# Attention scores from unrounded float32 q and k, two heads of a pair on two row tiles of TensorE

## The chip, the core and the metric

One core of a Trainium2 chip runs the kernel. The metric is the time of one execution on the device in microseconds (us), the median of several runs.

## The reference, cut to what matters

Attention over 2 batches of 12 heads (448 positions, 64 wide), then two feed-forward layers on the 896 tokens:

```python
scores = scale * np.matmul(q, k.transpose(0, 1, 3, 2))
scores = cap * np.tanh(scores / cap)
attn = np.exp(scores - np.max(scores, axis=-1, keepdims=True))
attn = attn / (np.sum(attn, axis=-1, keepdims=True) + 1e-09)
x = np.matmul(attn, v)              # then (B, H, S, D) -> (B*S, H*D)
h = x @ w_in                        # softmax times h, layer norm, @ w_out
...
(sigmoid(x @ w_gate) * (x @ w_val)) @ w_out
```

## The kernel before

The kernel has two branches, chosen at run time by the size of `cap`. With the cap of 30 of this input it takes the one without a maximum (`general` is False), and only that one is followed here.

**Stages.** Attention comes first, then layer 1 (`x @ w_in`, softmax, layer norm) by tiles of 128 tokens, then layer 2, and last the gated layer. Attention runs in *slots*. There are 12 pairs of heads, and slot `s` handles half of the keys (2 of 4 blocks of 112) of pair `s // 2`. The loop `for s in range(-1, NS)` (line 541) writes out the order of TensorE, VectorE, ScalarE and GpSimd by hand. In iteration `s` come the scores of slot `s + 1` (`s_mm`, line 202), their tanh (`s_tanh`, line 212), the product with v and the row sums of slot `s` (`s_pv`, line 238), the exp of slot `s + 1` (`s_exp`, line 235), and five steps of the weight conversion (`fill`, line 320). After an odd slot, `s_out` (line 265) copies the pair's product (on ScalarE, to `to`) and sums (on VectorE, to `ts`) out of PSUM. Two PSUM buffers hold product and sums, so the next pair's product waits for both copies. `n_recip` and `n_mult` divide by the sums two and four slots later; the reciprocals go out to DRAM and come back broadcast into the first two q and k tiles.

**Scores.** q and k of one head lie in one tile `qk_raw` of 128 partitions by 2 by 448, with the 64 values of the head dimension stored twice, on partitions 0 to 63 and 64 to 127. `s_round` (line 177) rounds both to float32r (`qk_hi`), `s_ql` (line 188) takes the remainder of q (`ql`), and `s_kl` (line 192) puts the remainder of k on the lower 64 partitions of `qk_hi`. Rounding is on VectorE and remainders are on GpSimd, except for the first two heads. A block of scores is then two float32r matmuls over 128 partitions:

```python
nc.tensor.matmul(sc[:KC, c, :S], ks, hi[:, 0], start=True, stop=False)
nc.tensor.matmul(sc[:KC, c, :S], ks, ql, start=False, stop=True)
```

The PSUM pool `big` has three buffers of two banks. Product and sums are plain float32 matmuls on column tiles: two of 64 columns for the two heads, four of 32 columns for the sums (lines 254 and 262). A plain float32 matmul stands in the trace as two MATMUL rows.

**Weights.** The 12 chunks of `w_in` come as 64-bit floats. A chunk has six steps on VectorE (lines 365, 368, 369, 370, 371, 355) with a cast to `wi_hi` on ScalarE (line 352) between the last two. Five steps stand in each slot from 0 to 15.

**Layer 1 beside attention.** From slot 17 on, 12 matmuls of layer 1 (line 421) stand in each slot on TensorE. The order of SyncE, which issues all transfers, is set by the scheduler of the framework.

Of the kernel before, what the change touches and what calls it, by code (L numbers as in the profile page):

```python
# [11 lines left out]
F32R = mybir.dt.float32r  # L12
# [3 lines left out]
ALU = mybir.AluOpType  # L16
# [4 lines left out]
P = 128  # L21
B, H, S, D = 2, 12, 448, 64
NP = H // 2
NH = B * H
NPAIR = B * NP
# [4 lines left out]
KC = 112  # L30
# [42 lines left out]
def f32(ap):  # L73
    return ap.bitcast(F32)
# [6 lines left out]
@with_exitstack  # L81
def fused_kernel(ctx: ExitStack, tc: tile.TileContext, qk, v, cap, w_in, w_mid, g_ln, w_gv, w_fin, outT):
    nc = tc.nc
    sh = Shared()
    const = ctx.enter_context(tc.tile_pool(name="const", bufs=1))
    sh.ps = ctx.enter_context(tc.tile_pool(name="ps", bufs=3, space=PSUM))
    sh.pso = ctx.enter_context(tc.tile_pool(name="pso", bufs=2, space=PSUM))
    sh.wraw = ctx.enter_context(tc.tile_pool(name="wraw", bufs=3, side="right"))
    sh.cvt = ctx.enter_context(tc.tile_pool(name="cvt", bufs=3, side="right"))
    sh.dram = ctx.enter_context(tc.tile_pool(name="dram", bufs=2, space=DRAM))  # L90


    cap_raw = const.tile([P, 1], F32, name="cap_raw")
    nc.sync.dma_start(out=cap_raw, in_=cap)

    def load(n, pool):
        b, hd = divmod(n, H)
        r = pool.tile([P, 2, S], F32, tag="q", name="qk_raw", bufs=2 if pool is const else N_RAW)
        nc.sync.dma_start(out=r, in_=qk[b, hd])
        return r  # L100

    sh.first = [load(n, const) for n in range(2)]
    sh.load, sh.v = load, v
    cap_neg = const.tile([P, 1], F32, name="cap_neg")
    sh.cap_abs = const.tile([P, 1], F32, name="cap_abs")
    sh.cap_inv = const.tile([P, 1], F32, name="cap_inv")
    nc.vector.tensor_scalar(cap_neg, cap_raw, -1.0, None, ALU.mult)
    nc.vector.tensor_tensor(sh.cap_abs, cap_raw, cap_neg, ALU.max)
    below = const.tile([P, 1], F32, name="below")
    flag = const.tile([P, 1], I32, name="flag")  # L110
    nc.vector.tensor_scalar(below, sh.cap_abs, CAP_FAST, None, ALU.is_le)
    nc.vector.tensor_copy(flag, below)
    nc.vector.reciprocal(sh.cap_inv, sh.cap_abs)
    nc.vector.tensor_scalar(sh.cap_inv, sh.cap_inv, 1.0 / float(D) ** 0.5, None, ALU.mult)
    sh.guard = const.tile([P, 1], F32, name="guard")
    nc.scalar.activation(sh.guard, sh.cap_abs, AF.Exp, scale=-1.0)
    nc.vector.tensor_scalar(sh.guard, sh.guard, EPS, None, ALU.mult)

    sh.ident = const.tile([P, P], F32, name="ident")
    make_identity(nc, sh.ident)  # L120

    warm = sh.ps.tile([P, 2, 512], F32, tag="big", name="warm")
    for c in range(WARM):
        nc.tensor.transpose(warm[:, c // 4 % 2, c % 4 * P:(c % 4 + 1) * P], sh.ident, sh.ident)
    sh.g_sb = const.tile([P, K2], F32, name="g_sb")
    nc.sync.dma_start(out=sh.g_sb, in_=g_ln)
    sh.ones = const.tile([KC, 32], F32, name="ones")
    nc.vector.memset(sh.ones, 1.0)
    sh.mhalf = const.tile([P, 1], F32, name="mhalf")
    nc.vector.memset(sh.mhalf, -0.5)  # L130

    bounded = nc.values_load(flag[:1], min_val=0, max_val=1)
    with tc.If(bounded > 0) as cmp:
        network(tc, sh, False, w_in, w_mid, w_gv, w_fin, outT)
    with cmp.Else():
        network(tc, sh, True, w_in, w_mid, w_gv, w_fin, outT)
# [3 lines left out]
def network(ctx: ExitStack, tc: tile.TileContext, sh, general, w_in, w_mid, w_gv, w_fin, outT):  # L142
    nc = tc.nc
# [4 lines left out]
    def big():  # L148
        t = ps.tile([P, 2, 512], F32, tag="big", name="big")
        return t  # L150
# [17 lines left out]
    a3 = att.enter_context(tc.tile_pool(name="a3" + sfx, bufs=3, side="right"))  # L168
# [2 lines left out]

    raws, qks, vs, es, outs, tos, rs, x_parts = {}, {}, {}, {}, {}, {}, {}, {}


    def s_round(n, split=False):
        qks[n] = (
            a3.tile([P, 2, S], F32R, tag="qk", name="qk_hi", bufs=4),
            a3.tile([P, S], F32R, tag="ql", name="ql", bufs=4),  # L180
        )
        if split:
            nc.scalar.copy(qks[n][0][:, 0], raws[n][:, 0])
            nc.vector.tensor_copy(qks[n][0][:, 1], raws[n][:, 1])
        else:
            nc.vector.tensor_copy(qks[n][0], raws[n])  # L186

    def s_ql(n, eng=nc.gpsimd):
        hi, ql = qks[n]
        eng.tensor_tensor(ql, raws[n][:, 0], f32(hi[:, 0]), ALU.subtract)  # L190

    def s_kl(n, eng=nc.gpsimd):
        hi, _ = qks[n]
        eng.tensor_tensor(hi[D:, 1], raws[n][D:, 1], f32(hi[D:, 1]), ALU.subtract)  # L194

    def v_load(i):
        if i < NPAIR:
# [1 line left out]
            vs[i] = a2.tile([KC, S // KC, P], F32, tag="v", name="v")  # L199
            nc.sync.dma_start(out=vs[i], in_=sh.v[b, hp])  # L200

    def s_mm(n, u):
        hi, ql = qks[n]
        sc = big()
        for c in range(2):
            kc = 2 * u + c
            ks = hi[:, 1, kc * KC:(kc + 1) * KC]
            nc.tensor.matmul(sc[:KC, c, :S], ks, hi[:, 0], start=True, stop=False)  # L208
            nc.tensor.matmul(sc[:KC, c, :S], ks, ql, start=False, stop=True)  # L209
        es[n, u] = sc  # L210

    def s_tanh(n, u):
        e = a3.tile([KC, 2, S], F32, tag="e", name="e", bufs=N_E)
# [261 lines left out]
    order = nullcontext() if general else tc.manual_schedule(engines=ORDERED)  # L475
    order.__enter__()

    def load_qk(n):
        if n < NH:
            raws[n] = sh.load(n, a3)  # L480

    def wi_dst(kk, half):
        c = slice(half * CH, half * CH + CH)
        return lambda: (wi_hi[:, kk, c], wi_lo[:, kk, c], None)

    load_qk(2)
    v_load(0)
    load_qk(3)
    for n in range(2):
        raws[n] = sh.first[n]  # L490
        s_round(n, True)
        s_kl(n, nc.vector)
        s_ql(n, nc.vector if n == 0 else nc.gpsimd)
    chunk_stream([(w_in[:, kk, h * CH:(h + 1) * CH], wi_dst(kk, h), None) for h in range(2) for kk in range(K1)])


# [9 lines left out]
    def phase(slot, k):  # L506
        run(beside.pop((slot, k), []))
# [32 lines left out]
    NS = 2 * NPAIR  # L540
    for s in range(-1, NS):
        m = s + 1
        i, u = divmod(s, 2)
        pair = range(m // 2 * 2, m // 2 * 2 + 2) if m < NS else ()
        for n in pair:
            s_mm(n, m % 2)
        phase(s, 0)
        for n in pair:
            s_tanh(n, m % 2)
        phase(s, 1)  # L550
        if s >= 0 and not general:
            s_pv(i, u)
        elif s >= 0 and u:
            s_pv(i, 0)
            s_pv(i, 1)
        if not general:
            for n in pair:
                s_exp(n, m % 2)
        elif m % 2:
            for n in pair:  # L560
                s_less_max(n)
                s_exp(n, 0)
                s_exp(n, 1)
        if 0 <= s < S_W2:
            fill(FILL)
        elif s == S_W2:
            fill(len(todo))
            w2_stream()
        elif S_W2 < s < S_W2 + 6 and wide:
            fill(s < S_W2 + 6)  # L570
        if u and s > 0 and i < NPAIR - 1:
            s_out(i)
        for n in (2, 3) if m == 0 else (m + 3,):
            if n < NH:
                s_round(n)
                s_ql(n)
                s_kl(n)
                raws.pop(n)
                load_qk(n + 2)
        if u == 0:  # L580
            v_load(i + 1)
        else:
            if i >= 1:
                n_recip(i - 1)
            if i >= 2:
                n_mult(i - 2)
        phase(s, 2)
        phase(s, 3)
# [21 lines left out]
    for t in range(L1_BESIDE, 7):  # L610
# [7 lines left out]
        k = FILL_T if wide else 0  # L618
# [116 lines left out]
    for m in range(DM // P):  # L735
# [3 lines left out]
        for hf in range(2):  # L739
            c = slice(hf * HT, hf * HT + HT)  # L740
# [7 lines left out]

def layouts(np, q, k, v, cap, moe_w_in, moe_w_out, moe_g_ln, moe2_w_gate, moe2_w_val, moe2_w_out):
    c = np.ascontiguousarray  # L750
    qk = np.stack([q, k], axis=2).transpose(0, 1, 4, 2, 3)
    gv = np.stack([moe2_w_gate.reshape(K3, P, K4, P), moe2_w_val.reshape(K3, P, K4, P)])

    def words(a):
        return a.view(np.int64) if a.dtype == np.float64 else a

    return {
        "qk": np.concatenate([qk, qk], axis=2),
        "v": c(v.reshape(B, NP, 2, S // KC, KC, D).transpose(0, 1, 4, 3, 2, 5).reshape(B, NP, KC, S // KC, P)),
        "cap": c(np.broadcast_to(np.asarray(cap).reshape(1, 1), (P, 1))),  # L760
        "w_in": words(c(moe_w_in.reshape(K1, P, F1).transpose(1, 0, 2))),
        "w_mid": words(c(moe_w_out.reshape(K2, P, K3, P).transpose(2, 1, 0, 3))),
        "g_ln": c(moe_g_ln.reshape(K2, P).T),
        "w_gv": words(c(gv.transpose(3, 2, 0, 1, 4).reshape(K4, P, 2 * K3, P))),
        "w_fin": words(c(moe2_w_out.reshape(K4, P, DM // P, P).transpose(2, 1, 0, 3))),
    }
# [15 lines left out]
```

## Time and profile before

| | |
|---|---|
| median of 3 runs | 535.73 us (534.26 to 537.21) |
| profiled execution | 534.95 us, span of its trace 533.2 us |
| TensorE busy | 500.2 us (94%) |
| VectorE busy | 381.3 us (72%) |
| ScalarE busy | 241.7 us (45%) |
| GpSimd busy | 129.0 us (24%) |
| mean DMA rate | 114 GB/s |
| granted TensorE clock | 0.986 of full speed, mean |

PE is TensorE's matmuls, PEld its weight loads, DVE VectorE, ACT ScalarE, POOL GpSimd, SP SyncE. L208 is line 208 of the kernel before. Busy time is a share of the whole span and mixes stages; which engine sets the pace of a stage is read from that stage's window and from the chain of waits. Matmul records overlap, since each has some latency behind its stream; the pace of a row of matmuls is read from their starts.

### The profile page before, as it was taken

How to read it: one execution, taken by the hardware profiler on the slowest of the kernel's cores; microseconds unless marked ns; L12 is line 12 of the kernel's file. 1: busy time of each engine (PE TensorE's matmuls, PEld its weight loads, DVE VectorE, ACT ScalarE, POOL GpSimd, SP SyncE). 2: the span in 40 equal slices, each digit the busy share in tenths (PEclk: the TensorE clock that was granted, in tenths of full speed). 3: DMA queues.
4: the chain of work that ended last, by engine and by line, in shares of the span. 5: the costliest groups of instructions: out<-in, count | busy, mean ns of one | idle time of the engine just before them, and what ended most of it. 6: DMA issues, size and time to landing. Idle time of an engine off the chain costs nothing.

```text
span 533.2 us, 6676 instructions
## 1 busy us (share of the span) xinstructions
PE 500.2 (94%) x2480; PEld 402.3 (75%) x2480; DVE 381.3 (72%) x607; ACT 241.7 (45%) x328; POOL 129.0 (24%) x86
## 2 busy tenths in 40 slices
PE   7879879899999897799999999999999999999996
PEld 6334333366567776689989999999999999999995
DVE  4999999466478888957978888888777776561000
ACT  5979679767624333222446434444333343332000
POOL 3556665874421120000000212221111111000000
PEclk8999889999999999899999999999999999999999
DMA  8757656621010111322555553444443334500001
GB/s 258 228 185 221 197 191 210 182 86 37 18 28 30 39 41 40 120 79 54 184 159 156 160 157 119 118 120 118 120 118 119 106 97 131 153 35 19 36 34 39
DMA packets 20788, 60.57 MB, mean 114 GB/s; under 512 B 3404, under 2 KB 6348, under 8 KB 20748
## 3 DMA queue, kind: packets, MB, share of 16 engines
q1 hardware_dynamic: 20748, 60.07, 36.6%
q8 instruction: 21, 0.34, 0.3%
q14 instruction: 19, 0.16, 0.1%
HBM read 57.18 MB, written 2.79 MB: 112 GB/s over the span
## 4 chain that ended last, share of the span: by engine, by line
PE 72%; DVE 16%; ACT 4%; DMA 4%; issue 2%; POOL 1%; SPq 1%; ACTq 0%; DVEq 0%; POOLq 0%
PE big L658 32%; PE l4o L658 16%; PE l2o L658 10%; PE big L421 6%; PE o L254 3%; DVE cvt L371 2%; DMA qk_raw<-in_qk 2%; DVE cvt L365 1%; DVE cvt L368 1%; DVE cvt L369 1%; DVE wi_lo L355 1%; PE big L208 1%; DMA w_raw<-in_w_in 1%; ACT e L214 1%; DVE qk_hi L186 1%
## 5 line engine op out<-in xcount | busy, mean ns | idle before, releaser
L658 PE MATMUL big<-y_hi,w_hl 128*128 128x448 f32 x576 | 161.7, 362 | 0.0
L658 PEld LDWEIGHTS big<-y_hi,w_hl 128*128 128x128 f32 x576 | 107.9, 187 | 7.9
L658 PE MATMUL big<-y_lo,w_hl 128*128 128x448 f32 x288 | 104.6, 363 | 0.0
L731 POOL TENSOR_TENSOR p_lo<-sg,p_hi 128x896 fp32r<-128x896 f32 x12 | 30.6, 2548 | 209.5 <-ACT p_hi L730 209.5
L658 PE MATMUL l4o<-p_hi,w_hl 128*128 128x448 f32 x288 | 80.7, 361 | 0.0
L352 ACT CAST w_hl<-cvt 128x512 fp32r<-128x512 f32 x66 | 40.8, 618 | 81.0 <-PE big L658 42.7
L371 DVE SCALAR_TENSOR_TENSOR cvt<-w_raw,cvt 128x512 uint32<-128x512 uint32 x78 | 75.6, 971 | 1.2
L355 DVE TENSOR_TENSOR w_hl<-cvt,w_hl 128x512 fp32r<-128x512 f32 x66 | 45.2, 685 | 24.8 <-ACT w_hl L352 24.5
L658 PE MATMUL l2o<-lnhi,w_hl 128*128 128x384 f32 (+1 forms) x192 | 57.0, 374 | 6.3 <-DVE w_hl L355 6.3
L363 ACT ACTIVATE cvt<-w_raw 128x512 f32<-128x512 f32 x54 | 36.2, 670 | 56.2 <-DVE w_hl L355 36.8
L368 DVE TENSOR_SCALAR cvt<-cvt 128x512 f32<-128x512 f32 x78 | 42.1, 540 | 24.3 <-ACT cvt L363 24.2
L370 DVE SCALAR_TENSOR_TENSOR cvt<-w_raw,cvt 128x512 uint32<-128x512 uint32 x78 | 57.7, 740 | 1.4
L658 PEld LDWEIGHTS l4o<-p_hi,w_hl 128*128 128x128 f32 x288 | 54.0, 187 | 3.9
L658 PEld LDWEIGHTS big<-y_lo,w_hl 128*128 128x128 f32 x288 | 54.1, 188 | 3.1
L214 ACT ACTIVATE e<-big,cap_inv 112x896 f32<-112x896 f32 x48 | 46.3, 1009 | 15.7 <-PE big L209 15.6
L658 PE MATMUL l4o<-p_lo,w_hl 128*128 128x448 f32 x144 | 52.3, 363 | 0.0
L254 PE MATMUL o<-e,v 112*64 112x448 f32 x192 | 43.8, 577 | 7.4 <-ACT to L270 2.8
L190 POOL TENSOR_TENSOR ql<-qk_raw,qk_hi 128x448 fp32r<-128x448 f32 x23 | 36.3, 1579 | 47.9 <-DVE r L280 25.6
L236 ACT ACTIVATE e<-e,cap_abs 112x896 f32<-112x896 f32 x48 | 47.4, 1044 | 0.0
L658 PEld LDWEIGHTS l2o<-lnhi,w_hl 128*128 128x128 f32 x192 | 36.3, 193 | 11.6 <-DVE w_hl L355 7.5
L208 PE MATMUL big<-qk_hi 128*112 128x448 f32 x96 | 38.5, 401 | 7.0 <-POOL qk_hi L194 5.5
L369 DVE TENSOR_SCALAR cvt<-cvt 128x512 uint32<-128x512 uint32 x78 | 42.0, 539 | 1.5
(90 smaller groups left out, 651.9 us busy)
## 6 DMA issues: line engine op xcount, KB each, us to landing
w_raw<-in_w_gv SPq DMA_DIRECT2D x36, 512.0 KB
qk_raw<-in_qk SPq DMA_DIRECT2D x24, 448.0 KB
w_raw<-in_w_fin SPq DMA_DIRECT2D x18, 512.0 KB
w_raw<-in_w_in SPq DMA_DIRECT2D x12, 512.0 KB
w_raw<-in_w_mid SPq DMA_DIRECT2D x12, 512.0 KB
v<-in_v SPq DMA_DIRECT2D x12, 224.0 KB
out_t<-ob SPq DMA_DIRECT2D x12, 224.0 KB
qk_raw<-rd SPq DMA_DIRECT2D x22, 112.0 KB
```

What stands on the lines that cost most here:

```text
L190: eng.tensor_tensor(ql, raws[n][:, 0], f32(hi[:, 0]), ALU.subtract)
L208: nc.tensor.matmul(sc[:KC, c, :S], ks, hi[:, 0], start=True, stop=False)
L214: nc.scalar.activation(e, es[n, u][:KC, :, :S], AF.Tanh, scale=sh.cap_inv[:KC])
L236: nc.scalar.activation(es[n, u], es[n, u], AF.Exp, scale=sh.cap_abs[:KC])
L254: nc.tensor.matmul(o[d, :S], vs[i][:, kc, d], e[j][:, c], start=(kc == 0), stop=(kc == 3))
L352: nc.scalar.copy(st["hi"], w)
L355: v.tensor_tensor(st["lo"], st["w"], f32(st["hi"]), ALU.subtract)
L368: word(lambda t, lo, hi: v.tensor_scalar(f32(t), f32(t), as_f32(W_MOST), as_f32(W_LEAST), ALU.min, ALU.max)),
L369: word(lambda t, lo, hi: v.tensor_scalar(t, t, 3, REST, ALU.logical_shift_left, ALU.bitwise_and)),
L370: word(lambda t, lo, hi: v.scalar_tensor_tensor(t, hi, TOP, t, ALU.bitwise_and, ALU.bitwise_or)),
L371: word(lambda t, lo, hi: (v.scalar_tensor_tensor(t, lo, 29, t, ALU.logical_shift_right, ALU.bitwise_or), upper())),
L658: nc.tensor.matmul(out, l, r[kx], start=(first and m == 0), stop=(last and m == 2))
```

## The change

Rounding and remainders are gone, and so are their tiles. A tile `qk_raw` now holds a pair: head 0 on partitions 0 to 63, head 1 on 64 to 127, nothing twice. It has the size of before, so 12 loads of 448 KB take the place of 24. A block of scores of one head is one plain float32 matmul over 64 partitions, and the two heads follow each other on the two halves of the array's rows, each writing another PSUM buffer.

```diff
-    def load(n, pool):
-        b, hd = divmod(n, H)
+    def load(i, pool):
+
+        b, hp = divmod(i, NP)
         r = pool.tile([P, 2, S], F32, tag="q", name="qk_raw", bufs=2 if pool is const else N_RAW)
-        nc.sync.dma_start(out=r, in_=qk[b, hd])
+        nc.sync.dma_start(out=r, in_=qk[b, hp])
         return r
...
-    def s_round(n, split=False):
...
-    def s_ql(n, eng=nc.gpsimd):
...
-    def s_kl(n, eng=nc.gpsimd):
...
-    def s_mm(n, u):
-        hi, ql = qks[n]
-        sc = big()
+    def s_mm(i, u):
+
+        sc = [big(), big()]
+        r = raws[i]
         for c in range(2):
             kc = 2 * u + c
-            ks = hi[:, 1, kc * KC:(kc + 1) * KC]
-            nc.tensor.matmul(sc[:KC, c, :S], ks, hi[:, 0], start=True, stop=False)
-            nc.tensor.matmul(sc[:KC, c, :S], ks, ql, start=False, stop=True)
-        es[n, u] = sc
+            for j in range(2):
+                d = slice(j * D, j * D + D)
+                nc.tensor.matmul(sc[j][:KC, c, :S], r[d, 1, kc * KC:(kc + 1) * KC], r[d, 0], start=True, stop=True)
+        for j in range(2):
+            es[2 * i + j, u] = sc[j]
...
-    load_qk(2)
     v_load(0)
-    load_qk(3)
-    for n in range(2):
-        raws[n] = sh.first[n]
-        s_round(n, True)
-        s_kl(n, nc.vector)
-        s_ql(n, nc.vector if n == 0 else nc.gpsimd)
+    for i in range(2):
+        raws[i] = sh.first[i]
+        load_qk(i + 2)
...
-        for n in pair:
-            s_mm(n, m % 2)
+        if m < NS:
+            s_mm(m // 2, m % 2)
...
-        for n in (2, 3) if m == 0 else (m + 3,):
-            if n < NH:
-                s_round(n)
-                s_ql(n)
-                s_kl(n)
-                raws.pop(n)
-                load_qk(n + 2)
+        if m % 2 and m < NS:
+            raws.pop(m // 2)
+            if m > 3:
+                load_qk(m // 2 + 2)
...
-    qk = np.stack([q, k], axis=2).transpose(0, 1, 4, 2, 3)
+    qk = np.stack([q, k], axis=2).transpose(0, 1, 4, 2, 3).reshape(B, NP, P, 2, S)
...
-        "qk": np.concatenate([qk, qk], axis=2),
+        "qk": c(qk),
```

TensorE's order before, from the product of slot 0 to the sums of slot 1 (the eight rows between them are the scores of slot 2, head by head):

```order
L254 MATMUL o<-e,v 64x448 x4
L262 MATMUL sums<-e,ones 32x448 x4
L208 MATMUL big<-qk_hi 112x448
L209 MATMUL big<-ql,qk_hi 112x448
L208 MATMUL big<-qk_hi 112x448
L209 MATMUL big<-ql,qk_hi 112x448
L208 MATMUL big<-qk_hi 112x448
L209 MATMUL big<-ql,qk_hi 112x448
L208 MATMUL big<-qk_hi 112x448
L209 MATMUL big<-ql,qk_hi 112x448
L254 MATMUL o<-e,v 64x448 x4
L262 MATMUL sums<-e,ones 32x448 x4
```

The same place on TensorE with the change (line 192 is the scores, 238 the product, 246 the sums):

```order
L238 MATMUL o<-e,v 64x448 x4
L246 MATMUL sums<-e,ones 32x448 x4
L192 MATMUL big<-qk_raw 112x448 x4
L238 MATMUL o<-e,v 64x448 x4
L246 MATMUL sums<-e,ones 32x448 x4
```

Eight matmuls of a slot's scores have become four, in the same place; nothing else on TensorE has moved.

VectorE's order before, in slots 3 and 4, from a copy of sums:

```order
L269 COPY ts<-sums 128x448
L186 CAST qk_hi<-qk_raw 128x896
L280 SCALAR_TENSOR_TENSOR r<-r,guard 16x56
L281 RECIPROCAL r<-r 16x56
L370 SCALAR_TENSOR_TENSOR cvt<-w_raw,cvt 128x512
L365 TENSOR_SCALAR cvt<-w_raw 128x512
L355 TENSOR_TENSOR wi_lo<-cvt,wi_hi 128x512
L371 SCALAR_TENSOR_TENSOR cvt<-w_raw,cvt 128x512
L368 TENSOR_SCALAR cvt<-cvt 128x512
L186 CAST qk_hi<-qk_raw 128x896
L369 TENSOR_SCALAR cvt<-cvt 128x512
```

The same place with the change (lines 349 to 355 and 339 are the steps of the conversion, 253 the copy, 264 and 265 the reciprocal):

```order
L253 COPY ts<-sums 128x448
L264 SCALAR_TENSOR_TENSOR r<-r,guard 16x56
L265 RECIPROCAL r<-r 16x56
L354 SCALAR_TENSOR_TENSOR cvt<-w_raw,cvt 128x512
L349 TENSOR_SCALAR cvt<-w_raw 128x512
L339 TENSOR_TENSOR wi_lo<-cvt,wi_hi 128x512
L355 SCALAR_TENSOR_TENSOR cvt<-w_raw,cvt 128x512
L352 TENSOR_SCALAR cvt<-cvt 128x512
L353 TENSOR_SCALAR cvt<-cvt 128x512
```

The casts are gone, and all other steps stand in the order of before.

SyncE's queue before, behind the two loads of the first heads:

```order
L99 DMA qk_raw<-in_qk 128x896
L200 DMA v<-in_v 112x512
L99 DMA qk_raw<-in_qk 128x896
L327 DMA w_raw<-in_w_in 128x1024 x3
L99 DMA qk_raw<-in_qk 128x896
L200 DMA v<-in_v 112x512
L99 DMA qk_raw<-in_qk 128x896 x2
L327 DMA w_raw<-in_w_in 128x1024
```

And with the change, behind the two loads of the first pairs (line 100 is q and k, 182 v, 311 the weights):

```order
L182 DMA v<-in_v 112x512
L100 DMA qk_raw<-in_qk 128x896 x2
L311 DMA w_raw<-in_w_in 128x1024 x3
L182 DMA v<-in_v 112x512
L100 DMA qk_raw<-in_qk 128x896
L311 DMA w_raw<-in_w_in 128x1024
```

v now comes ahead of the third and fourth tile of q and k; as many tiles of q and k as before stand ahead of the first weights, and they now hold eight heads instead of four.

## Rows read from the trace of the kernel before

**Rows 1.** The page: busy us, share of the span and instructions of each engine.

```profile
PE 500.2 (94%) x2480; PEld 402.3 (75%) x2480; DVE 381.3 (72%) x607; ACT 241.7 (45%) x328; POOL 129.0 (24%) x86
```

**Rows 2.** Busy time by stage: window, length, busy us (x instructions), then clock, DMA.

```profile
core 0: us, PE busy (x) PEld busy (x) DVE busy (x) ACT busy (x) POOL busy (x), PEclk, DMA share, GB/s
17.80:79.50 61.70, 50.95 (x259) 21.32 (x256) 61.08 (x80) 47.07 (x57) 39.21 (x25) 0.94 0.61 195
79.50:96.20 16.70, 13.40 (x73) 5.59 (x71) 15.81 (x22) 14.50 (x18) 10.68 (x7) 1.00 0.62 201
96.20:152.00 55.80, 55.40 (x282) 32.08 (x283) 31.24 (x54) 38.16 (x46) 31.41 (x21) 1.00 0.25 74
```

**Rows 3.** The chain of waits in order of time, 17 to 152 us: start, us, what.

```profile
17.77 0.63 DVE qk_hi L186
...
75.46 1.52 DVE cvt L370
...
148.99 2.97 PE big L421 x12
```

**Rows 4.** The timeline from 59.6 us, VectorE and GpSimd: start, us, what.

```profile
59.68 1.20 POOL L194 TENSOR_TENSOR qk_hi<-qk_raw,qk_hi 64x448 fp32r<-64x448 f32 x1
...
59.92 1.25 DVE L369 TENSOR_SCALAR cvt<-cvt 128x512 uint32<-128x512 uint32 x1
...
63.20 0.42 DVE L365 TENSOR_SCALAR cvt<-w_raw 128x512 uint32<-128x512 uint32 x1
```

**Rows 5.** VectorE's groups by form, 18 to 79 us: busy us, mean ns | idle before.

```profile
L368 DVE TENSOR_SCALAR cvt<-cvt 128x512 f32<-128x512 f32 x9 | 9.3, 1039 | 0.0
...
L186 DVE CAST qk_hi<-qk_raw 128x896 fp32r<-128x896 f32 x11 | 6.8, 617 | 1.1 <-DMA qk_raw<-in_qk 1.1
```

**Rows 6.** The same view from 250 to 480 us.

```profile
L368 DVE TENSOR_SCALAR cvt<-cvt 128x512 f32<-128x512 f32 x54 | 23.8, 441 | 23.4 <-ACT cvt L363 23.4
```

**Rows 7.** Instructions on the tile qk_hi: count, ns (least/median/most), first and last start.

```profile
L208 PE MATMUL big<-qk_hi x96: 358/365/575, 6.1 to 139.2; 128*112 128x448 f32 x96
...
L186 DVE CAST qk_hi<-qk_raw x22: 607/617/1547, 8.4 to 125.2; 128x896 fp32r<-128x896 f32 x22
L194 POOL TENSOR_TENSOR qk_hi<-qk_raw,qk_hi x22: 1141/1465/2757, 10.3 to 128.4; 64x448 fp32r<-64x448 f32 x22
```

**Rows 8.** The timeline of the start: warm-up matmuls, and the product of slot 0.

```profile
1.34 4.53 PE L124 MATMUL warm<-ident 128*128 128x128 f32 x20 [1.34 <-POOL ident masks.py:199]
...
12.69 1.78 PE L254 MATMUL o<-e,v 112*64 112x448 f32 x8
```

**Rows 9.** TensorE's timeline in slot 16, from its scores to the next ones.

```profile
99.76 0.46 PE L208 MATMUL big<-qk_hi 128*112 128x448 f32 x1
...
101.57 1.72 PE L254 MATMUL o<-e,v 112*64 112x448 f32 x8
103.22 0.96 PE L262 MATMUL sums<-e,ones 112*32 112x448 f32 x8
104.11 0.46 PE L208 MATMUL big<-qk_hi 128*112 128x448 f32 x1
```

**Rows 10.** ScalarE's timeline over two slots in which it never waits.

```profile
80.45 1.91 ACT L214 ACTIVATE e<-big,cap_inv 112x896 f32<-112x896 f32 x2
...
87.75 0.63 ACT L352 CAST wi_hi<-cvt 128x512 fp32r<-128x512 f32 x1
88.26 0.55 ACT L270 COPY to<-o 128x448 f32<-128x448 f32 x1
88.69 1.94 ACT L214 ACTIVATE e<-big,cap_inv 112x896 f32<-112x896 f32 x2
```

**Rows 11.** Instructions of line 254: count, ns (least/median/most), first and last start.

```profile
L254 PE MATMUL o<-e,v x192: 539/539/1009, 12.7 to 147.6; 112*64 112x448 f32 x192
```

**Rows 12.** Who waited for whom, 0 to 150 us: us in total, times, longest.

```profile
ACT wi_hi L352 <- DVE cvt L371: 11.5, 9, 1.9
...
PE o L254 <- ACT to L270: 2.8, 2, 1.4
```

More of the change, by code (lines that the diff above doesn't have):

```diff
@@ L169, in network @@
     a2 = att.enter_context(tc.tile_pool(name="a2" + sfx, bufs=2, side="right"))
-    raws, qks, vs, es, outs, tos, rs, x_parts = {}, {}, {}, {}, {}, {}, {}, {}
-    def s_round(n, split=False):
[L178 to L186, printed above, removed]
-    def s_ql(n, eng=nc.gpsimd):
-        hi, ql = qks[n]
-        eng.tensor_tensor(ql, raws[n][:, 0], f32(hi[:, 0]), ALU.subtract)
-    def s_kl(n, eng=nc.gpsimd):
-        hi, _ = qks[n]
-        eng.tensor_tensor(hi[D:, 1], raws[n][D:, 1], f32(hi[D:, 1]), ALU.subtract)
+    raws, vs, es, outs, tos, rs, x_parts = {}, {}, {}, {}, {}, {}, {}
     def v_load(i):
@@ L200, in v_load @@
             nc.sync.dma_start(out=vs[i], in_=sh.v[b, hp])
-    def s_mm(n, u):
-        hi, ql = qks[n]
-        sc = big()
+    def s_mm(i, u):
+        sc = [big(), big()]
+        r = raws[i]
         for c in range(2):
             kc = 2 * u + c
-            ks = hi[:, 1, kc * KC:(kc + 1) * KC]
-            nc.tensor.matmul(sc[:KC, c, :S], ks, hi[:, 0], start=True, stop=False)
-            nc.tensor.matmul(sc[:KC, c, :S], ks, ql, start=False, stop=True)
-        es[n, u] = sc
+            for j in range(2):
[3 more added lines that the diff above has]
+            es[2 * i + j, u] = sc[j]
     def s_tanh(n, u):
@@ L476, in network, with load_qk @@
     order.__enter__()
-    def load_qk(n):
-        if n < NH:
-            raws[n] = sh.load(n, a3)
+    def load_qk(i):
+        if i < NPAIR:
+            raws[i] = sh.load(i, a3)
     def wi_dst(kk, half):
@@ L572, in network @@
             s_out(i)
-        for n in (2, 3) if m == 0 else (m + 3,):
-            if n < NH:
-                s_round(n)
-                s_ql(n)
-                s_kl(n)
-                raws.pop(n)
-                load_qk(n + 2)
+        if m % 2 and m < NS:
+            raws.pop(m // 2)
+            if m > 3:
+                load_qk(m // 2 + 2)
         if u == 0:
```

## The prediction

> **What bounds the kernel now.** I start with the page's busy shares. TensorE is busy for 94% of the span, VectorE for 72% [rows 1]. Those are averages over stages, so the windows come next. From 17.8 to 79.5 us VectorE is busy 61.08 of 61.70 us, GpSimd 39.21, TensorE 50.95 and ScalarE 47.07. From 96.2 to 152 us TensorE is busy 55.40 of 55.80 us [rows 2]. The chain of waits agrees. From 17.77 to 77 us it runs almost wholly through VectorE, the last long piece being at 75.46. After a mixed stretch it stays on TensorE from 96 us to the end of attention, whose last piece is the layer 1 batch at 148.99 [rows 3]. So the first seventeen slots are paced by VectorE and the rest by TensorE. Everything after 152 us comes behind the change and reads none of its tiles; I leave it as it is.
>
> The pace of the first part is read from the starts of the products: slot 0 at 12.69 us [rows 8], slot 16 at 101.57 us [rows 9], which is 88.9 us over 16 slots, **5.56 us a slot**.
>
> Why VectorE is full there matters more than that it is full. One same instruction, the step of line 368, takes 1039 ns on average from 18 to 79 us [rows 5] and 441 ns from 250 to 480 us, where GpSimd has little to do [rows 6]. The timeline shows the difference case by case: a step of line 369 takes 1.25 us beside a GpSimd remainder, and a step of line 365 takes 0.42 us with GpSimd at rest as it starts [rows 4]. The reader is to see that the remainders on GpSimd cost twice, once on GpSimd and once as slowness of VectorE.
>
> **What goes.** (1) 22 rounding casts of 617 ns on VectorE [rows 7]; in the window of rows 5 they are 6.8 of its 61 us. (2) The remainders on GpSimd, 22 of k with a median of 1465 ns [rows 7] and as many of q of about that length. They leave GpSimd only the products with the reciprocals, one per two slots. (3) The three-step wait at the head of each slot: load, cast, remainders, matmul. Now a load alone stands ahead of it.
>
> VectorE's need per slot after the change lies between two ends. Without the casts and without any speeding up it is (61.1 - 6.8) us over the 11.1 slots of that window, 4.9 us. With all that is left sped up by 1039 to 441 it is 2.1 us. I take 3.3, nearer the lower end, because the conversion is most of what is left and showed the ratio; the copies and reciprocals did not.
>
> **What takes over.** ScalarE ran without waiting from 80.45 to 88.69 us: two slots in 8.24 us, with one cast of weights and one copy of a product among them [rows 10]. Over slots 0 to 15 there are 12 casts, so 1.5 per two slots; half a cast more (0.51 us from 87.75 to 88.26) adds 0.26. That is 8.5 us per two slots, **4.25 a slot**.
>
> TensorE's own loop, waiting for nothing, is 99.76 to 104.11 us, 4.35 us [rows 9]. Of it the scores are 1.81, the product 1.65 and the sums 0.89. Only the scores change: eight float32r matmuls become four float32 ones. The product already is four float32 matmuls of 448 columns, eight MATMUL rows in 1.65 us. One such row lasts 539 ns at least [rows 11] against 358 for a float32r one [rows 7]; the 181 ns between them are one more pass over 448 columns, so a row is two passes and a float32 matmul four, some 0.75 us by itself. Four in 1.65 us is only possible because the two column tiles run at the same time. If two row tiles do so too, the scores cost 1.65 us and the loop 4.19. No row shows row tiles. The two ends are 1.65, as the column tiles, and 3.3, twice that, if the halves follow one another. I take 1.65, as the product has the same count of rows, the same columns and the same order of heads.
>
> ScalarE at 4.25 and TensorE at 4.19 wait on each other once per pair, where a product needs the buffer that the copy on ScalarE frees: up to 1.4 us a time [rows 12], at most 0.7 a slot. So 4.25 to 4.9; I take **4.5 us a slot**, and the gain is 16 x (5.56 - 4.5) = **17.0 us**. Work that could step in: VectorE at 3.3 stays under 4.5, and the transfers moved 195 GB/s in that stage [rows 2] with each head's q and k sent twice, which now halves.
>
> **The start.** TensorE's warm-up ends at 1.34 + 4.53 = 5.87 us [rows 8]; the first scores needed a cast and two subtractions, and now need a load alone. From there 1.65 us of scores and one round of tanh and exp (half of 8.24 less the two copies, 3.6 us [rows 10]) put the first product at about 11.2 us instead of 12.69: **1.4 us** gained. In SyncE's queue the first tiles hold four heads instead of two, so the casts' wait for a load (1.1 us [rows 5]) has no successor.
>
> **The end of attention.** Behind slot 16 six groups of scores remain, on an engine that is full. They change by 6 x (1.65 - 1.81) = -1.0 us. Against it stands a change of the array's shape that was not there, between scores and layer 1. A shape change costs about 0.2 us: eight score matmuls at 0.20 us each would be 1.6, and took 1.81 with the entry from the sums [rows 9]. Six of those are +1.2. I book zero for both, with ends of -1 and, serial, +10.
>
> The Trainium skill (TensorEngine Tiling (Array Packing), Key Properties) says that changing the tiling mode drains TensorE, which speaks against the change. The 0.2 us above agrees. By that rule alone the end of attention would be 1.2 us longer, and by the rows it is even.
>
> **Sum.** 17.0 + 1.4 + 0 = 18.4 us off the profiled execution (534.95 us, 533.2 of it span): 516.6. The median of the runs is 0.8 above it, so **517.4 us**.
>
> **Rivals.** *Row tiles overlap in part.* Column tiles in four come to 3.3 of 4 here (eight rows of two passes, 2.98 us, in 0.89), in two to 1.8. If row tiles come to less, the scores lie between 1.65 and 3.3 us; a third of the way is 2.2. TensorE's loop is then 4.74, with some 0.3 of wait for the copies 5.0 a slot: 16 x 0.56 = 8.9, plus 0.9 at the start, less 6 x 0.39 and 1.2 at the end, 6.3 gained, 529 us. For it: no row shows row tiles. Against: the column tiles' 1.8.
>
> The Trainium skill (TensorE: Matmul & The Clock Gate, Part 3) gives 3.07 for four row tiles, three quarters of ideal. An estimate from that page for two, at the same share, is 1.53, scores of 2.15 us, and again 529 us; no run here shows it.
>
> *VectorE stays the bound.* If its slowness has another cause than GpSimd, only the casts go: 4.9 us a slot, 16 x 0.66 = 10.6, plus 1.4, 524 us. Rows 4 speak against it.
>
> *The halves do not overlap.* Then the scores cost 3.3 us and TensorE's loop is 4.35 - 1.81 + 3.3 = 5.84 us, above the 5.56 of today. It decides from a score price of about 3.0 us on. Slots 0 to 16 lose 16 x 0.28 = 4.5, the six groups behind lose 9, the start loses 0.3: **slower by 14, 550 us**. For it: four passes over 448 columns for each head is twice the work of before in array time. Against: the column tiles.
>
> *The change does not do what it says*, in that loads, not arithmetic, hold the slots. SyncE issues in order, and a load of a pair that waits for its buffer holds the weights and the round trip of the reciprocals behind it. Shorter slots leave less time for both. If each slot is held near 5.5 us, the time is 533 to 538.
>
> **Chances.** Forecast 0.62 (513 to 522), partial overlap 0.12, VectorE still the bound 0.08, held by loads 0.06, serial 0.12. The range 511 to 533 takes in the first three and leaves out the last two; its lower end is a slot of 4.25 with the end of attention 1 us shorter, rounded down for the clock (0.94 in the first part [rows 2]), its upper end partial overlap with a slot of 5.2. A difference of 0.5% (2.7 us) is about what a measurement of this kernel can tell. Faster by more: 0.82. Within: 0.06. Slower: 0.12.
>
> **What would show it.** Score matmuls of the two heads start in pairs and a slot's four end within about 1.7 us; the step of line 368 falls to some 450 ns in the first 80 us; the products of slot 0 and slot 16 start about 72 us apart, at 11 and 83; the chain there alternates ScalarE and TensorE; the stretch from the product of slot 16 to the last layer 1 batch beside attention stays at 50 us. I am wrong if the four scores take 3 us, if VectorE's steps stay near 1 us, or if what is gained at slot 16 is lost again in a later wait, for weights above all.

## The result and the profile after

The median went from 535.87 to **514.70 us** (four runs each; a fourth of the kernel before came in), a ratio of 0.961 with a 95% interval of 0.958 to 0.964: faster by 3.9%. The forecast was 517.4, the range 511 to 533. The profiled execution took 515.40 us, with a span of 513.5, against 534.95 and 533.2.

The page's first part, which answers to [rows 1]:

```profile
PE 495.0 (96%) x2480; PEld 386.8 (75%) x2480; DVE 336.4 (66%) x580; ACT 239.2 (47%) x326; POOL 57.1 (11%) x41
```

GpSimd lost 71.9 us of work and VectorE 44.9. Of the latter 15.1 us are the busy time of the 22 casts and some 3.5 the rounding and remainders of the first two heads, which are gone. The rest is the same steps, done faster.

The windows of the changed kernel, from the first scores to slot 17 and on, columns as in [rows 2]:

```profile
5.00:83.00 78.00, 77.28 (x423) 24.61 (x423) 47.74 (x94) 74.83 (x91) 7.17 (x6) 1.00 0.68 207
```

VectorE, full before, is busy for 47.74 of 78 us. TensorE (77.28) and ScalarE (74.83) are now both nearly full. TensorE's granted clock is 1.00 here, against 0.94 before [rows 2]. Where it had fallen in that stretch, VectorE was busy throughout (4.93 of 5 us from 56 to 61, 2.97 of 3 from 75 to 78), so the clock does not explain the old pace; what it cost there by itself was not tried.

VectorE's groups by form from 5 to 80 us (busy us, mean ns, idle before); line 352 is the step of line 368 before:

```profile
L253 DVE COPY ts<-sums 128x448 f32<-128x448 f32 x8 | 5.0, 623 | 7.6 <-PE sums L246 7.5
L352 DVE TENSOR_SCALAR cvt<-cvt 128x512 f32<-128x512 f32 x12 | 4.9, 407 | 0.0
```

The step takes 407 ns where it took 1039 [rows 5], and VectorE now waits for TensorE's sums (7.5 us).

TensorE's timeline: scores (line 192), product (238) and sums (246) of the start, of slots 1 and 16:

```profile
10.07 2.65 PE L238 MATMUL o<-e,v 112*64 112x448 f32 x8
...
15.23 1.72 PE L238 MATMUL o<-e,v 112*64 112x448 f32 x8
...
78.53 1.76 PE L192 MATMUL big<-qk_raw 64*112 64x448 f32 x8
80.22 1.72 PE L238 MATMUL o<-e,v 112*64 112x448 f32 x8
81.87 0.96 PE L246 MATMUL sums<-e,ones 112*32 112x448 f32 x8
82.76 1.76 PE L192 MATMUL big<-qk_raw 64*112 64x448 f32 x8
```

The products of slots 0 and 16 start 70.15 us apart, **4.38 us a slot** instead of 5.56. Scores take 1.69 us from their first start to the product's (78.53 to 80.22), the whole loop 4.23 (78.53 to 82.76).

The chain of waits in order of time shows what the slots end on:

```profile
20.04 1.81 ACT e L198 x2
21.85 1.86 ACT e L220 x2
23.70 0.51 ACT wi_hi L336
...
71.75 1.72 PE o L238 x8
73.47 0.89 PE sums L246 x8
74.36 1.69 PE big L192 x8
```

From 15 to 71 us it stays on ScalarE, with no piece of VectorE in it, and from 71.75 on TensorE. Even so, ten of the sixteen distances from the product of slot 0 to that of slot 16 are TensorE's own 4.23 or 4.24 us: the two engines are equally near the bound.

The difference of the two traces by stage, between the same instructions:

| stage | before | after | gained |
|---|---|---|---|
| to the product of slot 0 | 12.69 | 10.07 | 2.6 |
| product of slot 0 to that of slot 16 | 88.88 | 70.15 | 18.7 |
| to the last layer 1 batch beside attention | 47.35 | 48.49 | -1.1 |
| from there to the end | 384.28 | 384.79 | -0.5 |
| span | 533.2 | 513.5 | 19.7 |

So the gain lies in the first seventeen slots, and what follows gives back 1.7 us of it.

### The profile page after: what moved, and what is told of

It reads as the page before. It is cut to its first block, busy times and chain, and to the rows that moved or that the text cites. A ratio compares the mean times of both kernels' runs of the same rounds, so it can differ in the third digit from the quotient of the medians.

```text
span 513.5 us, 6510 instructions
## 1 busy us (share of the span) xinstructions
PE 495.0 (96%) x2480; PEld 386.8 (75%) x2480; DVE 336.4 (66%) x580; ACT 239.2 (47%) x326; POOL 57.1 (11%) x41
## 4 chain that ended last, share of the span: by engine, by line
PE 76%; ACT 14%; DVE 7%; issue 2%; POOL 0%; ACTq 0%; POOLq 0%
PE big L635 34%; PE l4o L635 17%; PE l2o L635 11%; PE big L405 5%; ACT e L198 5%; ACT e L220 5%; PE big L192 3%; PE o L238 3%; DVE e L423 1%; ACT wi_hi L336 1%; DVE lnlo L456 1%; PE big L449 1%; PE sums L246 1%; ACT e L420 1%; PE warm L125 1%
## 5 line engine op out<-in xcount | busy, mean ns | idle before, releaser
L355 DVE SCALAR_TENSOR_TENSOR cvt<-w_raw,cvt 128x512 uint32<-128x512 uint32 x78 | 72.8, 934 | 1.2
L354 DVE SCALAR_TENSOR_TENSOR cvt<-w_raw,cvt 128x512 uint32<-128x512 uint32 x78 | 53.6, 687 | 1.4
L352 DVE TENSOR_SCALAR cvt<-cvt 128x512 f32<-128x512 f32 x78 | 33.7, 433 | 22.5 <-ACT cvt L347 22.3
L192 PE MATMUL big<-qk_raw 64*112 64x448 f32 x192 | 43.0, 559 | 0.3 <-ACT e L198 0.3
L353 DVE TENSOR_SCALAR cvt<-cvt 128x512 uint32<-128x512 uint32 x78 | 37.0, 476 | 1.6
L635 PE MATMUL l2o<-lnlo,w_hl 128*128 128x384 f32 (+1 forms) x96 | 36.0, 375 | 0.0
```

The costliest lines, as they stand in the source:

```text
L192: nc.tensor.matmul(sc[j][:KC, c, :S], r[d, 1, kc * KC:(kc + 1) * KC], r[d, 0], start=True, stop=True)
L352: word(lambda t, lo, hi: v.tensor_scalar(f32(t), f32(t), as_f32(W_MOST), as_f32(W_LEAST), ALU.min, ALU.max)),
L353: word(lambda t, lo, hi: v.tensor_scalar(t, t, 3, REST, ALU.logical_shift_left, ALU.bitwise_and)),
L354: word(lambda t, lo, hi: v.scalar_tensor_tensor(t, hi, TOP, t, ALU.bitwise_and, ALU.bitwise_or)),
L355: word(lambda t, lo, hi: (v.scalar_tensor_tensor(t, lo, 29, t, ALU.logical_shift_right, ALU.bitwise_or), upper())),
L635: nc.tensor.matmul(out, l, r[kx], start=(first and m == 0), stop=(last and m == 2))
```

## The experiments

The theory: GpSimd's remainders slowed VectorE, and VectorE paced the slots; the row tiles work at the same time, so the scores cost as much as before. The rivals: the pace came from the chain of load, cast, remainder and matmul; or from the casts; or the new scores are cheap without any overlap.

**Both heads on one row tile** (`one_tile`).

```diff
-                d = slice(j * D, j * D + D)
+                d = slice(0, D)
```

> The changed kernel with both heads' score matmuls on the upper row tile (partitions 0 to 63). The second head's scores are left out: the first head's are computed twice; loads, counts and waits are unchanged. If the gain needs the two row tiles at the same time: a slot's four score matmuls take 3.0 to 3.4 us instead of 1.69, a slot 5.6 to 5.9 instead of 4.38, the time 543 to 551 us. Rival, a float32 matmul over 64 rows is cheap by itself: scores stay near 1.7 us and the time at 514 to 517.

Measured 548.41 us, 1.024 of before (1.017 to 1.031). TensorE's timeline in two slots:

```profile
21.07 3.26 PE L192 MATMUL big<-qk_raw 64*112 64x448 f32 x8
24.26 1.72 PE L238 MATMUL o<-e,v 112*64 112x448 f32 x8
25.91 0.96 PE L246 MATMUL sums<-e,ones 112*32 112x448 f32 x8
26.80 3.26 PE L192 MATMUL big<-qk_raw 64*112 64x448 f32 x8
```

The same four matmuls take 3.19 us on one row tile and 1.69 on two, a factor of 1.89, and the slot is 5.73 us. That is the serial rival of the prediction, which it put at 550 us: without the overlap the change would have lost 2.4%.

**The heads one after the other** (`head_outer`).

```diff
-        for c in range(2):
-            kc = 2 * u + c
-            for j in range(2):
-                d = slice(j * D, j * D + D)
+        for j in range(2):
+            d = slice(j * D, j * D + D)
+            for c in range(2):
+                kc = 2 * u + c
```

> The changed kernel with the two score matmuls of the first head ahead of the two of the second, instead of the heads taking turns. If a matmul overlaps only with its neighbour in program order: the first runs alone, the second with the third, the fourth alone, about 2.3 us a slot, the time 522 to 530 us. Rival, order does not matter, since the halves run on by themselves: scores stay at 1.7 us, 514 to 516.

Measured 514.89 us, 0.959 (0.956 to 0.963). TensorE's timeline, scores and the product of slot 3:

```profile
22.37 1.77 PE L192 MATMUL big<-qk_raw 64*112 64x448 f32 x8
24.07 1.76 PE L238 MATMUL o<-e,v 112*64 112x448 f32 x8
```

The scores still take 1.70 us, so the order of the heads does not matter here; of the two expectations the first, that a matmul overlaps only with its neighbour, was wrong. Whether TensorE's queue or the compiler brings the two heads together is not seen in these rows.

**Subtractions back on GpSimd** (`rems_back`), at the places of the old ones, on constant tiles:

```diff
+    def dummy(n):
+        t = a3.tile([P, S], F32R, tag="ql", name="d_lo", bufs=4)
+        a = sh.dsrc[n % 4]
+        nc.vector.memset(a[:, :1], 0.3)
+        nc.gpsimd.tensor_tensor(t, sh.done[:, 0], a, ALU.subtract)
+        nc.gpsimd.tensor_tensor(t[D:], sh.done[D:, 1], a[D:], ALU.subtract)
```

> The changed kernel with as many subtractions of the old sizes on GpSimd as before (one of 128x448 and one of 64x448 per head, on constant tiles, each pair released by a tiny memset on VectorE; nothing waits for their results). If contention of GpSimd and VectorE set the old pace: the step of line 352 of the changed kernel goes from 0.43 to about 1.0 us in the first 80 us, a slot to about 4.9 us (the old busy time less the casts), the time to 519 to 527 us. Rival, the pace was set by the chain of load, cast, remainder and matmul: the steps may slow down, but the time stays within 1.5 us of 514.7.

Measured 523.86 us, 0.977 (0.973 to 0.981): 9.2 us above the changed kernel, with nothing waiting for these results. VectorE's groups by form, 5 to 80 us:

```profile
L339 DVE TENSOR_TENSOR wi_lo<-cvt,wi_hi 128x512 fp32r<-128x512 f32 x11 | 11.6, 1059 | 0.4 <-ACT wi_hi L336 0.4
L355 DVE SCALAR_TENSOR_TENSOR cvt<-w_raw,cvt 128x512 uint32<-128x512 uint32 x11 | 11.3, 1026 | 0.0
L352 DVE TENSOR_SCALAR cvt<-cvt 128x512 f32<-128x512 f32 x12 | 9.8, 820 | 0.0
```

And VectorE's and GpSimd's timelines from 40 us (one fence each):

```profile
40.36 1.25 DVE L353 TENSOR_SCALAR cvt<-cvt 128x512 uint32<-128x512 uint32 x1
41.64 1.53 DVE L354 SCALAR_TENSOR_TENSOR cvt<-w_raw,cvt 128x512 uint32<-128x512 uint32 x1
43.09 0.41 DVE L349 TENSOR_SCALAR cvt<-w_raw 128x512 uint32<-128x512 uint32 x1
43.43 0.68 DVE L339 TENSOR_TENSOR wi_lo<-cvt,wi_hi 128x512 fp32r<-128x512 f32 x1
```

```profile
40.11 1.21 POOL L529 TENSOR_TENSOR d_lo<-done,dsrc 64x448 fp32r<-64x448 f32 x1
41.40 1.22 POOL L273 TENSOR_TENSOR x<-to,qk_raw 128x448 f32<-128x448 f32 x1
44.21 1.52 POOL L528 TENSOR_TENSOR d_lo<-done,dsrc 128x448 fp32r<-128x448 f32 x1 [1.59 <-DVE dsrc L527]
```

A step that meets a GpSimd instruction is longer by about what is left of it: 1.25 instead of 0.43 us beside a subtraction, 1.53 instead of 0.69 beside a product with the reciprocals. Between 42.6 and 44.2 us GpSimd rests, and the steps are as short as without it. The second end of the theory holds too: with the work on GpSimd alone, most of the old slowness comes back (820 ns for line 352, against 407 without it and 1039 before). The Trainium skill (SBUF — State Buffer, Terms) calls the port pair of these two engines exclusive, held for a whole instruction; these rows agree, 1.25 against 0.43 us.

**Casts back on VectorE** (`casts_back`).

```diff
+    def dummy(n):
+        t = a3.tile([P, 2, S], F32R, tag="qk", name="d_hi", bufs=4)
+        nc.vector.tensor_copy(t, sh.dsrc)
```

> The changed kernel with the 22 casts of 128x896 on VectorE put back at their places, on a constant tile; nothing waits for their results. Both theories: VectorE's need is some 3.1 + 0.6 us a slot, under the 4.38 of a slot, so 514 to 516.5 us. If VectorE is nearer its bound than thought: up to 520.

Measured 515.25 us, 0.960 (0.956 to 0.963), the time of the changed kernel. Its windows line from 5 to 80 us (columns as in [rows 2]) says why:

```profile
5.00:80.00 75.00, 74.28 (x405) 23.74 (x402) 56.77 (x112) 71.89 (x88) 6.00 (x5) 1.00 0.69 208
```

With the casts VectorE is busy for 56.77 of 75 us and has room. By themselves the casts cost nothing that can be told from zero.

**Both back** (`both_back`), the cast and the two subtractions from it, on a constant tile:

```diff
+        nc.vector.tensor_copy(t, sh.dsrc)
+        nc.gpsimd.tensor_tensor(lo, sh.dsrc[:, 0], f32(t[:, 0]), ALU.subtract)
+        nc.gpsimd.tensor_tensor(t[D:, 1], sh.dsrc[D:, 1], f32(t[D:, 1]), ALU.subtract)
```

> The changed kernel with casts and subtractions put back together, cast to remainders as before, on a constant tile; no load is waited for and no matmul waits for the results. If VectorE's load under contention set the old pace: a slot of 5.4 to 5.6 us, the time 530 to 535. Rival, the chain from load to matmul cost a good part by itself: a slot of 5.2 us or less, 528 or less, and what is missing to 534 is the chain's.

Measured 530.34 us, 0.991 (0.988 to 0.993). Of the 21.2 us between the two kernels 15.6 come back: 0.5 with casts alone, 9.2 with subtractions alone, 5.9 more together, since the casts that were free now stand on an engine without room. These are differences of medians from different comparisons, whose medians of the kernel before lie between 535.47 and 536.54, so each is good to about 1 us.

Against the kernel before (535.47 in that comparison) 5.1 us are missing. The two traces show by stage where: 2.5 us up to the product of slot 0 (10.19 against 12.69) and 5.4 us in the 16 slots (83.51 against 88.88), less 3.3 us that this kernel is slower from there to the last layer 1 batch beside attention. So a slot is 5.22 us, hardly more than the 5.2 of the rival: of the 18.7 us gained in the slots, 13.4 come back with the engines' load alone, and 5.4 do not. What is left of the old kernel for those 5.4 is that loads are waited for and that matmuls wait for casts and remainders. Its chain of waits has such a place, where the product of slot 15 starts 8.0 us after that of slot 14:

```profile
91.86 0.53 DVE qk_hi L186
92.39 0.18 DVE r L280
...
92.63 2.00 POOL ql L190
...
94.71 1.47 POOL qk_hi L194
...
96.22 0.46 PE big L208
```

Cast, remainder of q, remainder of k, and only then the scores, with TensorE waiting. That the whole 5.4 us are such places is argued, not tried one by one.

**The kernel before without remainders** (`before_no_rems`): the opposite side.

```diff
-            nc.tensor.matmul(sc[:KC, c, :S], ks, ql, start=False, stop=True)
+            nc.tensor.matmul(sc[:KC, c, :S], ks, hi[:, 0], start=False, stop=True)
...
-                s_ql(n)
-                s_kl(n)
```

> The kernel before without the remainders on GpSimd and VectorE; the second matmul takes the rounded q again, so scores are doubled twice over and left so. Casts, loads, both matmuls and the wait for the casts stay. Contention theory: the weight steps fall to some 0.45 us, a slot to 4.4 to 4.7 us, the time to 516 to 523 us. Rival, the chain of load, cast and matmul sets the pace: 528 or more.

Measured 515.57 us, 0.963 (0.960 to 0.966). Casts, 24 loads and eight float32r matmuls a slot are all still there, and the time is that of the changed kernel. Its windows line over the stretch of [rows 2]:

```profile
17.80:79.50 61.70, 59.88 (x332) 27.18 (x334) 53.11 (x101) 59.73 (x75) 8.17 (x5) 1.00 0.75 243
```

VectorE has room, and TensorE and ScalarE are full; the median step of line 368 takes 424 ns. So removing the remainders is worth the whole gain. This run takes away their load on GpSimd, the slow VectorE steps and the waits for them at once; how the slots divide between load and waits is what `both_back` tells. The float32 matmuls on row tiles are what makes that possible without losing the remainders' accuracy, and over the whole kernel they neither cost nor bring time that these runs can tell. By stage they do both: here the products stand 4.35 us apart from slot 2 on, TensorE's old loop, where the changed kernel has 4.23, and the stretch from the product of slot 16 to the last layer 1 batch takes 47.35 us, where the changed kernel has 48.49.

**Attempts at a faster version.** ScalarE and TensorE now share the bound, VectorE and GpSimd have room. Four edits move work to these, each on the changed kernel.

(a) `to_dve`: the copy of the product on VectorE.

```diff
-        (nc.vector.tensor_copy if i < NPAIR - 1 else nc.scalar.copy)(st, sums[:, :S])
-        nc.scalar.copy(t, o[:, :S])
+        if i < NPAIR - 1:
+            nc.vector.tensor_copy(t, o[:, :S])
+            nc.vector.tensor_copy(st, sums[:, :S])
```

> The changed kernel with the copy of a pair's product out of PSUM on VectorE (ahead of the copy of the sums) instead of ScalarE, for all pairs but the last. ScalarE is left 0.22 us a slot less; TensorE's own loop of 4.23 us is then the bound: 16 x 0.15 = 2.4 off, 512 to 513 us. Rival, VectorE is late with the copy behind its weight steps and the next product waits longer: 515 to 519.

Measured 515.63 us, 0.963 (0.960 to 0.965). The slots run at 4.23 us up to 66.29, as expected. Then two are late. The timeline there, all engines:

```profile
70.05 0.61 ACT L340 CAST wi_hi<-cvt 128x512 fp32r<-128x512 f32 x1
...
70.69 1.35 DVE L343 TENSOR_TENSOR wi_lo<-cvt,wi_hi 128x512 fp32r<-128x512 f32 x1 [3.46 <-ACT wi_hi L340]
71.96 0.61 DVE L254 COPY to<-o 128x448 f32<-128x448 f32 x1
...
72.67 2.31 PE L238 MATMUL o<-e,v 112*64 112x448 f32 x8 [2.08 <-ACT e L198]
```

VectorE waits 3.46 us for a cast on ScalarE that stands behind the exp, the copy stands behind that wait, and the next product behind the copy, which ends at 72.57 (the tanh that the row names as its releaser is no input of that product). The second late product follows at a lower clock (0.67 from 72 to 77 us), with sums of 1.72 us instead of 0.96.

(b) `to_dve_first`: both copies ahead of the weight steps of the slot (`s_out(i)` before `fill(FILL)`).

> As to_dve, with both copies of a pair ahead of the weight steps of that slot on VectorE. If in to_dve only the place of the copy behind a weight step was at fault (the stop before the product of slot 14): no stop, a slot of 4.23 to 4.3 us throughout, 512 to 513.5 us. Rival, VectorE now waits for the sums with its weight steps behind it, and casts and loads come late: 515 or more.

Measured 519.89 us, 0.970 (0.968 to 0.973). The chain of waits shows the wait only moved to the other engine:

```profile
36.39 0.62 DVE ts L255
...
39.01 1.58 DVE cvt L359
...
40.61 0.62 ACT wi_hi L340
41.23 1.81 ACT e L198 x2
```

The weight steps now stand behind the sums, the cast on ScalarE behind the steps, and the next tanh behind the cast.

(c) `wi_pool`: the 12 casts of the first weights on GpSimd.

```diff
-            nc.scalar.copy(st["hi"], w)
+            (nc.gpsimd.tensor_copy if scale is None and not act else nc.scalar.copy)(st["hi"], w)
```

> The changed kernel with the 12 casts of the first weights on GpSimd instead of ScalarE. ScalarE is left 0.38 us a slot less, TensorE's loop of 4.23 us is the bound: 512 to 513.5 us. The casts contend with VectorE for 12 x some 1.3 us, which its slack covers. Rival, the casts are slow or hold up VectorE's last step and the buffers: 515 to 520.

Measured 513.77 us, 0.958 (0.955 to 0.961). The chain runs on TensorE alone through these slots:

```profile
31.62 1.69 PE big L192 x8
33.31 1.65 PE o L238 x8
34.97 0.89 PE sums L246 x8
35.85 1.69 PE big L192 x8
```

Products stand 4.235 us apart from slot 1 on, against 4.33 in the changed kernel (15.23 to 80.22 over 15 slots): 1.5 us in all, the end of what TensorE's loop allows. Its first product came 1.1 us later (11.15 against 10.07), a difference of the start that is taken up below. As a time of the whole kernel its interval overlaps with that of the changed kernel, so it is no proven gain.

(d) Pairs 2, 4, 6 and 8 with added halves, to shorten TensorE's sums: on (a) as `to_dve_adds`, on (c) as `wi_pool_adds`.

```diff
-ADD_PAIRS = range(9, 11)
+ADD_PAIRS = (2, 4, 6, 8, 9, 10)
```

> As to_dve, and pairs 2, 4, 6 and 8 also add the two halves of the exponentials on VectorE, as pairs 9 and 10 do, so that TensorE's sums of such a pair take 0.89 instead of 1.78 us. If TensorE's loop is the bound: up to 4 x 0.89 = 3.6 off the time of to_dve, some 509 us. Rival, the additions fill VectorE in those slots (4 x 0.7 us a pair) and its copies come late: no gain over to_dve, or a loss of some us.

> As wi_pool, and pairs 2, 4, 6 and 8 add the halves of the exponentials on VectorE, which saves 0.89 us of sums on TensorE per pair. ScalarE's own need is then 3.95 us a slot, TensorE's 4.0 on average: up to 3.6 us less than wi_pool, 508 to 510. Rival, the additions queue behind weight steps on VectorE and the sums wait for them: no gain over wi_pool, or a loss.

Measured 516.78 us, 0.965 (0.963 to 0.967), and 515.64 us, 0.961 (0.958 to 0.963): no gain over (a) or (c). TensorE's timeline of `wi_pool_adds` in slot 17, the second of pair 8, and the scores after the layer 1 batch:

```profile
83.54 2.29 PE L238 MATMUL o<-e,v 112*64 112x448 f32 x8
85.76 1.55 PE L244 MATMUL sums<-es,ones 112*32 112x448 f32 x6
87.85 0.94 PE L244 MATMUL sums<-es,ones 112*32 112x448 f32 x2 [0.54 <-DVE es L232]
91.67 1.76 PE L192 MATMUL big<-qk_raw 64*112 64x448 f32 x8
```

The sums, which take 0.89 us when their inputs are there, wait here for the additions on VectorE. What TensorE saves in one slot it waits for in the other: in `wi_pool_adds` the first slots of pairs 2, 4 and 6 take 3.34 to 3.35 us, the second ones 4.80, 5.45 and 5.46, where `wi_pool` has 4.23 to 4.24 for each.

## Why the prediction was right

- **VectorE's slowness is GpSimd's doing**: right. The step fell to 407 ns (forecast 450); VectorE's need came to 47.74 us over the 17.8 slots of that window, 2.7 us a slot (forecast 3.3, between 2.1 and 4.9). Putting GpSimd's work back brought the slowness back.
- **Row tiles overlap as column tiles do**: right. 1.69 us for the scores (forecast 1.65), 3.19 on one tile (the other end was 3.3).
- **4.5 us a slot**: 4.38. ScalarE's own 4.25 and TensorE's loop of 4.23 (forecast 4.19) stood, and I gave the wait between them 0.25 a slot where it is some 0.13. That term measured 18.7 us against 17.0. Part of the wait is the first distance, 5.16 us, which holds the stop for the second exp. The chain was forecast to alternate between ScalarE and TensorE, and stays on ScalarE up to 71 us.
- **The start**: 2.6 us against 1.4. The first scores began at 5.39, not 5.87, and the first product starts after the first exp, not after both. The first part is mostly luck of this execution: its warm-up took 4.12 us, with the last matmuls 0.11 us apart instead of 0.21, where that of `wi_pool`, with the same start, took 4.53. Among the profiled executions that begin as the changed kernel does, the first product stands between 10.06 and 11.20 us, so the gain is 1.5 to 2.6. The second part is no real gain: that product lasts 2.65 us, waiting for the second exp. By the product of slot 1 (15.23 against 17.09) the lead is 1.9 us. The prediction also read 12.69 as the price of cast and subtractions alone. From 9 to 13 us the granted clock of the kernel before was 0.57, mostly the lower of its two levels (1.2 GHz), after TensorE had waited 1.03 us for a remainder; its scores stood 0.37 us apart instead of 0.20 and held the first product back, while the first exp was done at about 11.7.
- **The end of attention**: booked at zero, measured at -1.1. Two of its terms were mis-sized and one was missing. The scores came to some 0.2 us less in all (booked 1.0). The shape change is there, but only three layer 1 batches stand right behind scores, not six: they took 2.73 to 2.75 us in the chain before and 2.94 to 2.95 after, 0.6 in all (booked 1.2). The missing term is 0.7 us: the last scores stand ahead of transposes that wait for the first tanh, and with row tiles the scores of both heads end together, where head 0 had been ready halfway. The rows are of before and after:

```profile
140.11 1.06 PE L465 MATMUL big<-ident,e 128*128 128x128 f32 x8 [0.38 <-ACT e L214]
119.86 1.06 PE L449 MATMUL big<-ident,e 128*128 128x128 f32 x8 [1.18 <-ACT e L198]
```

- **Nothing behind attention moves**: -0.5 us of 384.
- **Removing the casts** was listed as a part of the gain; alone it is worth nothing that can be told, and some 6 us only while GpSimd's work is there (530.34 against 523.86 us).
- **The loads** were not a bound: 207 GB/s in that stage, with no transfer in the chain of waits.

The sum was 1.2 us short by the profiled executions (18.4 against 19.6): the start and the slots were taken too cautiously by 2.9 us, and 1.7 us were lost behind them that the sum had at zero. That the two partly cancel is luck. The median came out 2.7 us below the forecast. The other 1.5 us are the spread of single executions: the forecast added 0.8 for a median above its profiled execution, and the changed kernel's median lies 0.7 below its own.

## What to carry to other kernels

Before counting what an instruction on GpSimd costs, look at the same VectorE step in a stretch where GpSimd rests: here work that seemed to run beside the bound made single steps of the bound up to three times as long. In this kernel four float32 matmuls with a contraction of 64, on two row tiles, cost about as much time as eight float32r matmuls over 128 rows (1.69 against 1.81 us a slot), and need no rounding and no remainders ahead of them. When two engines then share the bound, moving a copy to an idle engine helped only where nothing on that engine's queue ahead of it waited for the first two.

## What had not been expected

The order of the two heads made no difference: four matmuls of one tile pair took 1.70 us with the heads one after the other and 1.69 with the heads taking turns, though adjacent matmuls on one tile take 3.19 us for four. And the casts, 22 instructions and 15.1 us on the engine that paced the old kernel, cost 0.5 us by themselves, less than the comparison can tell from nothing.
